# A joined state-space convolution and multi-query attention kernel: the start reordered, two rounds of scores over three key blocks put ahead of two projection steps, allowance 1.80

## The chip, the cores and the metric

The kernel runs on one core of a Trainium2 chip. The time is device microseconds for one execution of the whole program, and the figure that counts is the median of several runs of the same program. Lower is better.

## The reference

Two independent results are computed and put side by side. The first (A) is a long convolution: a kernel K of 2048 taps is generated for each of 576 channels from complex exponentials over 128 states, the input u is convolved with it, and a skip term is added. The second (B) is attention with 32 query heads of width 18 and one shared key and value head, over 2048 positions.

```python
P = jnp.exp(logdA[:, :, None] * l[None, None, :])
K = jnp.einsum("dn,dnl,dn->dl", Cc, P, dB).real
...
y = irfft2(rfft2(pad(u)) * rfft2(pad(K)))[..., :L] + u * Dskip
...
q = (x @ wq).reshape(B, S, 32, 18)
k = x @ wk
v = x @ wv
scores = einsum("bhqd,bkd->bhqk", q, k) * 18 ** -0.5
o = einsum("bhqk,bkd->bhqd", softmax(scores), v)
b = o.reshape(B, S, 576) @ wo
return concatenate([a, b], axis=-1)
```

## The kernel before

Attention is the spine. The 2048 queries are cut into four chunks of 512, the heads into 16 pairs, the keys into 16 blocks of 128. One element of the list `pairs` is (chunk c, group g, key block kb, member j): head pair 2g+j against key block kb. For each element TensorE (PE) makes a tile of scores (`scores`, line 516: two matmuls, one per head, 128 keys by 512 queries), and ScalarE (ACT) turns it into exponentials P (`exponentials`, lines 525 and 527). For each two elements (one step, both members of a key block) PE multiplies P with the values (`product`, line 817: four matmuls into `ops`). There are 1024 elements and 512 steps. Scores go out in rounds of NS = 3 elements, because three PSUM tiles hold them; ten P tiles (NP) lie between exponentials and products. Line 525 is the first group of chunk 0, which uses a bias.

Queries and keys are made as fp16 high and low parts with 55 rows for a pair member (18 high, 18 high, 18 low and one row for a bound). The queries of a pair stand in `aug`, the keys in `kaug`, 512 columns for each chunk of positions. `place` writes six small DMAs of 18 rows to fill one chunk of `kaug`.

The convolution is a second list of work (class Conv) whose VectorE (DVE) and PE instructions are put between those of attention. DVE makes tables of powers, PE generates K from them (`kg`), both u and K go through a transform on PE (`hu`, `hk`, `lu`, `lk`), DVE multiplies, PE transforms back (`iy`), and SP stores the result `outa`. There are twelve chunks of channels; chunk k+1's first half (`front`) runs beside chunk k's second half (`back`).

The order of PE, ACT and DVE is the order in which the program emits instructions (`manual_schedule`); the tile framework orders the other engines' queues, GpSimd's (POOL) among them. The emission follows a planner in `main`: a Clock keeps a rough account of each engine's time, and after each round `fill` places other work on PE: query projections, output projections and convolution. How far the convolution may run is an allowance: with `work` as the DVE time that the planner has booked for it, `lag = step * RATE - work`; below -20 nothing more is emitted, and a positive lag lets DVE be booked up to 1 us further ahead. `lags` puts the convolution ahead of the query projections while `work < step * PACE`.

The start is in `setup` (lines 234 to 344). It loads the first chunk of x (`x0`, five pieces of 128 input channels), the other three chunks (`xr`, five pieces), the query weights `wq[0]`, the key and value weights `wkv` and tables. Then:

- "first": the queries of heads 0 to 6 and the keys of chunk 0, five accumulation steps over k.
- ACT makes `h1` (high part), DVE `l1` (low part). `place(0)` and twelve DMAs from line 322 fill `kaug` chunk 0 and `aug[0]`, `aug[1]`.
- `rest(k)`, k = 0 to 4: the keys of chunks 1 to 3 and the last queries into "second", the values into "vps". Between the first of them the bias is made (`small`).
- Three matmuls over zeros (`spare`, from `wo`).
- DVE makes `h2` and `l2` from "second", and `place(1)` fills `kaug` chunk 1, on SP and POOL; then the values are copied (`vt`).

In `main`, after the first round of scores (r = 0), `settle` transposes the values into `v_sb`, places `kaug` chunks 2 and 3 on SP, loads `wq[2]` to `wq[4]` and starts the convolution's larger loads. After the third round (r = 6) `bounds` makes the limits `kmx` of the key blocks, which the later queries wait for.

Of the kernel before, what the change touches and what calls it, by code (L numbers as in the profile page):

```python
# [17 lines left out]
P = 128  # L18
# [3 lines left out]
DH = 18  # L22
SCALE = DH ** -0.5
NCH = 4
CT = 512
# [17 lines left out]
NS = 3  # L43
NP = 10


RATE = 1.84
PACE = 1.79
# [147 lines left out]
class Attention:  # L196
# [36 lines left out]
    def setup(self, tp, conv):  # L233
# [29 lines left out]
        nc.scalar.dma_start(self.wq[0], a["wq"][0])  # L263
        nc.sync.dma_start(wkv, a["wkv"])
        for k in range(5):
            n = DT[k][1]
            nc.sync.dma_start(x0[:n, k, :], a["xT"][0, :n, k, :])
        nc.scalar.dma_start(self.sel, a["sel"][:, 0:45])
        nc.scalar.dma_start(spread[:, 0:140], a["sel"][:, 45:185])
        for k in range(5):  # L270
# [5 lines left out]
        self.load_wq(1)  # L276
# [11 lines left out]
        p1, small, spare = p1[:, 0, :], small[:, 0, :], small[:, 1, 0:256]  # L288
        V.memset(self.wo[:, 0, 0:384], 0.0)
# [26 lines left out]
        self.place(0, h1, l1, 96, (nc.sync, nc.sync))  # L316
        for pr in range(2):
            for row, src in ((0, h1), (18, h1), (36, l1)):
                for j in range(2):
                    h, b = 2 * pr + j, 64 * j + row  # L320
                    q = nc.sync if pr and row == 36 else nc.gpsimd
                    q.dma_start(self.aug[pr][b:b + 18, :], src[h * DH:h * DH + DH, :])
# [18 lines left out]
        V.tensor_copy(vt, pv)  # L341
        V.tensor_reduce(self.km[:, 4:5], p2, axis=AX.X, op=ALU.max, apply_absolute_value=True)
        V.tensor_scalar(self.km[:, 4:5], self.km[:, 4:5], QS, None, op0=ALU.mult)
        self.vt = vt
# [412 lines left out]
    def main(self, conv, flag):  # L757
# [9 lines left out]
        pairs = [(c, g, kb, j) for c in range(NCH) for g in range(8) for kb in range(16) for j in range(2)]  # L767
        state = dict(credit=0.0, filled=0.0)
# [41 lines left out]
        def product(n):  # L810
            nonlocal o_ps
            c, g, kb, _ = pairs[2 * n]
# [3 lines left out]
            for j in range(4):  # L816
                nc.tensor.matmul(o_ps[32 * j:32 * j + 32, :], self.v[:, kb, :], pts[2 * n + j // 2][:, j % 2, :],  # L817
                                 start=(kb == 0), stop=(kb == 15), tile_position=(0, 32 * j))
            K.pe(0.88, done[2 * n + 1] + 0.1, self.o_free if kb == 0 else 0.0)
# [749 lines left out]
```

## Time and profile before

| what | value |
|---|---|
| median of 3 runs | 1157.36 us (1155.91 to 1157.46) |
| the profiled execution | 1158.43 us |
| its span, first to last instruction | 1156.7 us |
| PE busy | 1083.0 us (94%) |
| ACT busy | 998.6 us (86%) |
| DVE busy | 995.8 us (86%) |
| POOL busy | 141.5 us (12%) |
| mean granted TensorE clock | 0.993 |

The span is one execution; the 1.7 us between it and the time of that execution lie outside the first and last instruction. PE time is counted by matmul records. An fp32 matmul makes two records, an fp16 one makes one. Four matmuls of 32 output columns that stand side by side in the array are four instructions and run together, so that their records overlap.

### The profile page before, as it was taken

The numbers are of one execution on the slowest core, as the hardware profiler recorded it, in microseconds if no ns is written. First come the engines' busy times: TensorE is split into PE (matmuls) and PEld (weight loads), VectorE is DVE, ScalarE is ACT, GpSimd is POOL, SyncE is SP. The second block draws the span as 40 slices with busy tenths as digits, with TensorE's granted clock in tenths as the row PEclk, the third lists the DMA queues.
The fourth block names the chain that finished last, engine by engine and source line by source line (L and its number), as shares of the span: only waits on it lengthen the run. The fifth ranks groups of instructions, "written<-read, shape, count | busy, mean of one in ns | idle before, by whom it ended". The sixth has DMA issues, their size and how long they took to land.

```text
span 1156.7 us, 33067 instructions
## 1 busy us (share of the span) xinstructions
PE 1083.0 (94%) x13886; PEld 393.1 (34%) x13886; DVE 995.8 (86%) x1739; ACT 998.6 (86%) x1052; POOL 141.5 (12%) x257
## 2 busy tenths in 40 slices
PE   6999899999999999899999999989999999999997
PEld 1333333324334333323333333334323333323323
DVE  3788996998998998898899798997898899799683
ACT  3889998888888998998898989887999989899992
POOL 5321322022022000001022000001050000000000
PEclk9999999999999999999999999999999999999999
DMA  7412331114123102112222302102122200311101
GB/s 226 140 46 73 125 119 50 52 42 143 36 74 101 40 28 93 58 40 87 82 85 77 104 21 74 48 29 91 46 84 77 87 30 29 105 48 47 58 29 58
DMA packets 58751, 83.37 MB, mean 72 GB/s; under 512 B 14467, under 2 KB 34679, under 8 KB 58085
## 3 DMA queue, kind: packets, MB, share of 16 engines
q1 hardware_dynamic: 47173, 73.39, 19.2%
q0 software_dynamic: 10848, 7.37, 2.5%
q8 instruction: 111, 1.82, 0.6%
q10 hardware_dynamic: 576, 0.43, 0.2%
q14 instruction: 43, 0.35, 0.1%
HBM read 46.59 MB, written 33.85 MB: 70 GB/s over the span
## 4 chain that ended last, share of the span: by engine, by line
PE 59%; DVE 21%; ACT 12%; issue 6%; DMA 1%; POOL 1%; ACTq 0%; DVEq 0%; POOLq 0%
PE ops L817 24%; PE s L516 15%; ACT P L527 11%; PE op L193 5%; PE q L408 4%; DVE tab L119 4%; PE iy L193 3%; DVE ks L119 3%; PE kg L1253 3%; DVE acc L119 2%; DVE t L119 2%; PE hu L193 1%; PE hk L193 1%; DVE fr L119 1%; PE fin L193 1%
## 5 line engine op out<-in xcount | busy, mean ns | idle before, releaser
L527 ACT ACTIVATE P<-s 128x1024 f32<-128x1024 f32 x992 | 934.6, 1033 | 113.8 <-PE s L516 111.5
L817 PE MATMUL ops<-P,v_sb 128*32 128x512 f32 x4096 | 510.4, 599 | 8.1 <-DVE o L123 7.8
L516 PE MATMUL s<-aug,kaug 55*128 55x512 f16 x2048 | 308.2, 381 | 37.3 <-ACT P L527 33.4
L516 PEld LDWEIGHTS <-kaug 55*128 55x128 f16 x2048 | 91.0, 94 | 372.3 <-issue 326.7
L817 PEld LDWEIGHTS ops<-P,v_sb 128*32 128x32 f32 x4096 | 117.0, 110 | 164.8 <-issue 128.3
L458 POOL DMA_DIRECT2D qd<-qh x116 | 65.6, 572 | 309.6 <-DVE qh L127 307.0
L408 PE MATMUL q<-x,wq_sb 128*32 128x256 f32 x1360 | 83.7, 382 | 0.1
L193 PE MATMUL op<-wo_sb,oT 126*32 126x288 f32 (+1 forms) x1080 | 78.5, 416 | 2.6 <-DVE ob L123 1.4
L119 DVE TENSOR_TENSOR tab<-tab,tt 128x576 f32<-128x576 f32 (+1 forms) x72 | 59.1, 821 | 1.4
L119 DVE TENSOR_TENSOR tab<-tab 128x576 f32<-128x576 f32 (+1 forms) x72 | 58.8, 817 | 0.0
L119 DVE TENSOR_TENSOR tab<-fr,dif 128x576 f32<-128x576 f32 (+1 forms) x72 | 58.8, 817 | 0.0
L119 DVE TENSOR_TENSOR tt<-fr,sum 128x576 f32<-128x576 f32 (+1 forms) x72 | 58.8, 817 | 0.0
L119 DVE TENSOR_TENSOR tab<-sum,fr 128x576 f32<-128x576 f32 (+1 forms) x72 | 58.8, 817 | 0.0
L123 DVE COPY ksb<-kg 128x192 f32<-128x192 f32 x48 | 17.5, 364 | 46.9 <-PE kg L1253 46.6
L408 PEld LDWEIGHTS q<-x,wq_sb 128*32 128x32 f32 x1360 | 39.4, 109 | 38.5 <-issue 13.9
L119 DVE TENSOR_TENSOR acc<-acc,pt 128x1728 f32<-128x1728 f32 (+2 forms) x36 | 48.7, 1352 | 0.1
L119 DVE TENSOR_TENSOR pt<-us,ks 128x1728 f32<-128x1728 f32 (+2 forms) x36 | 48.4, 1351 | 0.1
L1162 POOL MEMSET fr<- 128x192 f32 x24 | 11.9, 580 | 294.0 <-DVE tt L119 192.2
L193 PEld LDWEIGHTS op<-wo_sb,oT 126*32 126x32 f32 (+1 forms) x1080 | 30.6, 110 | 44.2 <-issue 18.3
L525 ACT ACTIVATE P<-s,bias 128x1024 f32<-128x1024 f32 x32 | 32.8, 1123 | 12.9 <-PE s L516 12.7
L1253 PEld LDWEIGHTS kg<-tab 128*32 128x32 f32 x2304 | 35.7, 110 | 22.7 <-DVE ksb L123 7.6
L1253 PE MATMUL kg<-tab 128*32 128x64 f32 x2304 | 41.8, 220 | 1.2 <-DVE tab L119 0.8
(160 smaller groups left out, 1022.4 us busy)
## 6 DMA issues: line engine op xcount, KB each, us to landing
od<-o SPq DMA_DIRECT2D x31, 256.0 KB
aug<-qd SPq DMA_DIRECT2D x124, 55.0 KB
u<-u SPq DMA_DIRECT2D x12, 384.0 KB
kd<-ksb SPq DMA_DIRECT2D x12, 384.0 KB
kt<-kd SPq DMA_DIRECT2D x48, 96.0 KB
outa<-u SPq DMA_DIRECT2D x12, 384.0 KB
pw<-pw SPq DMA_DIRECT2D x8, 528.0 KB
oT<-od SPq DMA_DIRECT2D x16, 252.0 KB
```

Source lines behind the costliest of these rows:

```text
L119: return self.v.tensor_tensor(out, *a, **k)
L123: return self.v.tensor_copy(out, *a, **k)
L193: nc.tensor.matmul(ps[j:e], w[:, j:e], x, start=start, stop=stop, tile_position=(0, j))
L408: nc.tensor.matmul(ps[o, 256 * f:256 * f + 256], w[:, k, i], xt[:, k, x], start=(k == 0), stop=(k == 4), tile_position=(0, 32 * j))
L458: q.dma_start(qd[h:h + n, row + d:row + d + nd, cs], src[i1:i1 + n * nd, :cs.stop - cs.start])
L516: nc.tensor.matmul(ps[:, j, :], self.kaug[r, kb * P:(kb + 1) * P], t[r, :], start=True, stop=True)
L525: nc.scalar.activation(pt, ps, AF.Exp, bias=self.bias, scale=SCALE / QQ)
L527: nc.scalar.activation(pt, ps, AF.Exp, scale=SCALE / QQ)
L817: nc.tensor.matmul(o_ps[32 * j:32 * j + 32, :], self.v[:, kb, :], pts[2 * n + j // 2][:, j % 2, :], start=(kb == 0), stop=(kb == 15), tile ...
L1162: nc.gpsimd.memset(t[:, :, 0:NF:8], one)
L1253: nc.tensor.matmul(ps[32 * g:32 * g + 32, d, :], t[:, :32], t[:, 32:], start=(j == 0), stop=(j == 1), tile_position=(0, 32 * g))
```

## The change

The changed program does the following.

- Loads: `wq[0]` goes first on ACT's queue, the first piece of `x0` first on SP's, then `wkv`, then the other pieces of `x0` in two DMAs with all 128 rows (the padding rows come from the host's array, and the memset of them goes). The convolution's first parameters follow on ACT's queue and on POOL's, `sel` and `spread` on POOL's.
- `xr` pieces 0 to 2 are loaded as before, pieces 3 and 4 and `wq[1]` only after the DMAs that place `h1` and `l1`; a memset of one element on DVE ahead of each makes it wait there.
- Four matmuls over zeros (`WARM`) stand at the start, the three `spare` ones go. The memsets of `ring` move from POOL to DVE.
- The low part's two DMAs into `kaug` chunk 0 go to ACT's queue; all twelve `aug` DMAs go to POOL's.
- `rest(3)` moves behind the first round of scores, `rest(4)` and the making and placing of `h2`, `l2`, `vt` (`keys_rest`) behind the second. `settle` comes after the third round, `bounds` after the fifth.
- The first six elements of `pairs` are reordered: key blocks 0, 1, 2 of pair 0, then of pair 1. `place`, `member` and `exp` keep the products in step with it.
- Three more parts of the convolution's first chunk are emitted in `setup` (`conv.begin(3)`).
- POOL's order, too, is that of the program.
- RATE 1.84 becomes 1.80, PACE 1.79 becomes 1.75.

```diff
-RATE = 1.84
-PACE = 1.79
+WARM = 4
+RATE = 1.80
+PACE = 1.75
...
-        nc.gpsimd.memset(x0[64:, 4, :], 0.0)
+        V.memset(self.wo[:, 0, 0:384], 0.0)
         nc.gpsimd.memset(xr[64:, 4], 0.0)
-        for j in range(2):
-            nc.gpsimd.memset(self.ring[j], 0.0)
+        nc.scalar.dma_start(self.wq[0], a["wq"][0])
+        nc.sync.dma_start(x0[:, 0, :], a["xT"][0, :, 0, :])
+        nc.sync.dma_start(wkv, a["wkv"])
+        nc.sync.dma_start(x0[:, 1:3, :], a["xT"][0, :, 1:3, :])
+        nc.sync.dma_start(x0[:, 3:5, :], a["xT"][0, :, 3:5, :])
         conv.early()
...
+        for k in range(3):
+            load_rest(k)
...
+        warm = self.bank(256, "warm")
+        for _ in range(WARM):
+            matmul4(nc, warm, self.wo[:, 0, 0:P], self.wo[:, 0, P:P + 256])
+        for j in range(2):
+            V.memset(self.ring[j], 0.0)
...
-        self.place(0, h1, l1, 96, (nc.sync, nc.sync))
+        for row, src in ((0, h1), (36, h1), (18, l1)):
+            for j in range(2):
+                b = 64 * j + row
+                (nc.scalar if row == 18 else nc.sync).dma_start(self.kaug[b:b + 18, 0:CT], src[96:96 + 18, :])
...
+        for k in range(3, 5):
+            V.memset(xr[0:1, k, :, 0:1], 0.0)
+            load_rest(k)
+        V.memset(self.wq[1][0:1, 0, 0:1], 0.0)
+        self.load_wq(1)
...
-        for k in range(2, 5):
-            rest(k)
-        for _ in range(3):
-            matmul4(nc, spare, self.wo[:, 0, 0:P], self.wo[:, 0, P:P + 256])
+        rest(2)
+        conv.begin(3)
+        self.rest_of, self.p2_p3, self.vt = rest, (p2, pv), vt
+
+    def keys_rest(self):
...
+        pairs[0:6] = pairs[0:6:2] + pairs[1:6:2]
...
             if r == 0:
+                self.rest_of(3)
+                K.t += 1.9
+                continue
+            if r == NS:
+                self.rest_of(4)
+                self.keys_rest()
+                K.t += 1.9
+                continue
+            if r == 2 * NS:
                 self.settle(conv)
-            if r == 2 * NS:
+            if r == 4 * NS:
                 self.bounds()
...
-        with tc.manual_schedule(engines={mybir.EngineType.PE, mybir.EngineType.Activation, mybir.EngineType.DVE}):
+        with tc.manual_schedule(engines={mybir.EngineType.PE, mybir.EngineType.Activation, mybir.EngineType.DVE, mybir.EngineType.Pool}):
```

More of the change, by code (lines that the diff above doesn't have):

```diff
@@ L287, in setup @@
         p1, small = (self.ps_s.tile([P, 2, CT], F32, tag="s", name=n) for n in ("first", "small"))
[L288 to L289 removed]
+        p1, small, spare = p1[:, 0, :], small[:, 0, :], None
         p2 = self.bank(CT, "second")
@@ L320, in setup @@
                     h, b = 2 * pr + j, 64 * j + row
-                    q = nc.sync if pr and row == 36 else nc.gpsimd
-                    q.dma_start(self.aug[pr][b:b + 18, :], src[h * DH:h * DH + DH, :])
+                    nc.gpsimd.dma_start(self.aug[pr][b:b + 18, :], src[h * DH:h * DH + DH, :])
+        for k in range(3, 5):
[3 more added lines that the diff above has]
+        self.load_wq(1)
         V.tensor_scalar(self.km[:, 0:1], ab[:, 0:1], spread[:, 139:140], None, op0=ALU.mult)
@@ L767, in main @@
         pairs = [(c, g, kb, j) for c in range(NCH) for g in range(8) for kb in range(16) for j in range(2)]
+        pairs[0:6] = pairs[0:6:2] + pairs[1:6:2]
+        place = {x: i for i, x in enumerate(pairs)}
+        member = lambda i: 16 * (8 * pairs[i][0] + pairs[i][1]) + pairs[i][2]
+        exp = lambda n, j: place[n // 128, n // 16 % 8, n % 16, j]
         state = dict(credit=0.0, filled=0.0)
@@ L840, in main @@
             for i in new:
-                while (i - NP) // 2 >= behind:
+                while i >= NP and member(i - NP) >= behind:
                     product(behind)
@@ L845, in main @@
                 c, g, kb, j = pairs[i]
-                pts[i] = self.exponentials(i, c, 2 * g + j, kb, *ss[i], read.get((i - NP) // 2, 0.0))
+                pts[i] = self.exponentials(i, c, 2 * g + j, kb, *ss[i], read.get(member(i - NP), 0.0) if i >= NP else 0.0)
                 done[i] = K.a
@@ L1115, in powers @@
         if g == 0:
-            for k in (1, 2):
-                self.load(k)
             yield "v", K.v + 0.3, False
@@ L1185, in factors @@
         w = self.coefficients(k)
-        if k > 0:
-            self.load(k + 2)
+        for j in (k + 2,) if k else (1, 2):
+            self.load(j)
         if k + 1 == BURSTS[g][1]:
```

37 lines of the change are left out of this document (19 added, 18 removed).

## The prediction

> **What bounds the kernel now.** I read the page first, then a table of windows, then the timeline and the chain of waits of the start.
>
> ```profile
> span 1156.7 us, 33067 instructions
> ...
> PE 1083.0 (94%) x13886; PEld 393.1 (34%) x13886; DVE 995.8 (86%) x1739; ACT 998.6 (86%) x1052; POOL 141.5 (12%) x257
> ```
>
> ```profile
> 0.00:14.00 14.00, 6.03 (x44) 1.39 (x48) 3.42 (x9) 3.91 (x5) 4.72 (x11) 1.00 0.80 253
> 14.00:26.30 12.30, 10.81 (x114) 3.42 (x106) 4.86 (x13) 2.69 (x4) 8.27 (x17) 1.00 0.77 232
> 26.30:36.00 9.70, 7.56 (x54) 3.01 (x50) 5.51 (x27) 9.16 (x9) 7.55 (x14) 0.91 0.28 76
> 46.00:60.00 14.00, 13.90 (x172) 4.80 (x168) 11.86 (x20) 12.12 (x13) 5.59 (x10) 1.00 0.35 105
> ...
> 200.00:400.00 200.00, 189.27 (x2530) 70.28 (x2524) 184.23 (x344) 176.01 (x188) 32.82 (x60) 1.00 0.23 71
> ```
>
> The columns are the window, its length, busy time of PE, weight loads, DVE, ACT and POOL, the granted clock, the DMA share and GB/s. Later PE is full: 13.90 of 14 us, then 95% of 200. In the first 36 us it idles 8.0, 1.5 and 2.1 us, and an idle microsecond there is one at the end, as the work left is the same. So I follow the start to a landmark, the end of the fourth round of scores, where two products are done and PE is full:
>
> ```profile
> 36.55 1.37 PE L516 MATMUL s<-aug,kaug 55*128 55x512 f16 x6
> ```
>
> It began at 36.55 and ended at 37.92. Before it:
>
> ```profile
> 0.75 4.01 DMA pos_sb<-pos
> ...
> 4.78 2.79 DMA x<-xT
> ...
> 7.62 1.07 PE first L294 x3
> ...
> 9.55 0.85 PE first L294 x3
> ...
> 11.32 0.43 PE first L294 x3
> ...
> 13.55 0.61 ACT keys L311
> ```
>
> ```profile
> 14.74 4.02 POOL L322 DMA_DIRECT2D aug<-keys  x8 [9.41 <-ACT keys L311]
> ...
> 23.18 0.63 PE L298 MATMUL second<-xr,wkv_sb 128*32 128x512 f32 x3 [0.25 <-DMA xr<-xT]
> ...
> 24.30 0.69 DVE L127 TENSOR_SCALAR keys<-second 128x512 f16<-128x512 f32 x1 [5.75 <-PE second L294]
> ...
> 24.89 1.50 PE L193 MATMUL small<-wo_sb 128*32 128x256 f32 x24
> ...
> 26.33 1.04 PE L516 MATMUL s<-aug,kaug 55*128 55x512 f16 x6
> ...
> 26.78 9.16 ACT L525 ACTIVATE P<-s,bias 128x1024 f32<-128x1024 f32 x9 [9.72 <-PE s L516]
> ```
>
> The first x piece is issued at 4.78, held by the landing of another load, and lands at 7.57. "First" then runs to 13.5, its rows 0.85 apart until 10.4 and 0.43 apart later (two rows to a k). The last pieces of the other chunks arrive at 23.18, the zeros take 1.50, and the first scores go at 26.33. From there ACT sets the pace: nine exponentials in 9.16, and PE waits for its PSUM tiles.
>
> **The change part by part.** *x first.* In the first 40 us the loads are limited by what the DMA engines move (GB/s for each microsecond, so KB):
>
> ```profile
> GB/s 0 4 41 128 334 297 296 293 330 356 317 360 391 391 385 383 383 391 281 203 258 220 156 23 43 72 94 56 67 40 31 63 34 302 84 18 52 20 169 293
> ```
>
> Before, 1007 KB are issued up to the first x piece (24+48+96 parameters, 11 pos, 160 wkv, 320 wq, 92 tables, 256 x). The row adds up to that at 6.7, and the piece lands at 7.57, 0.9 later. Now 736 KB (x, wq, wkv) suffice: 5.8 + 0.9 = 6.7. All of x with those small loads is 2031 KB: 9.9 + 0.9 = 10.8, and the two steps of k that arrive last take 2 x 0.86, so "first" ends at 12.5 instead of 13.5. Bounds: 11.0 (6.7 and ten rows of 0.43), 13.5 (nothing gained). I take 1.0 sooner, by the bytes. The WARM matmuls lie in the 7.6 us that PE idles at the start; they bring the 0.43 pace from the first step, which the bytes then hide.
>
> *h1 and aug.* h1 is then done at 13.1 and l1 1.3 later. POOL issues at 0.5 each (4.02 for eight), four high rows from 13.7, then two low: the sixth, the last that pair 0 needs, at 16.2. Time to landing:
>
> ```profile
> DMA to landing us min/median/max: 4.2/6.4/7.0
> ```
>
> ```profile
> DMA to landing us min/median/max: 1.7/1.9/3.4
> ```
>
> The first row is POOL's aug under the load of xr, the second its kaug later, when the engines move little. xr pieces 0 to 2 are now 2031 + 2304 KB, which the GB/s row reaches at 16.1; so the sixth flies as the load ends. Between 1.7 and 7.0 I take 3.0: it lands at 19.2. rest(2) needs xr 2 at 17.0 (16.1 + 0.9) and is done at 18.8, within that. First scores at 19.2 rather than 26.33.
>
> The Trainium skill (page "DMA: Bandwidth & Descriptors", section "Anatomy of one DMA — SWDGE (gpsimd) path") puts a DMA of POOL at about 2.0 us and its bytes over 436 GB/s, so 2.0 for 18 KB; the trace agrees for kaug (1.9) and not for aug (6.4). By that rule the scores would start 1.0 us sooner.
>
> *From there on.* Three scores take 1.0, a rest 1.8 (twice the matmuls of a k of "first", so four rows of 0.43). Scores to 20.2; rest(3) to 22.0 (its xr lands near 19 if the rate holds, SP issues it after four kaug at 0.7 from 13.1); scores of member 1 to 23.0; rest(4) to 24.8. Then h2 and l2 as before, 24.8 to 26.2, and `kaug` chunk 1:
>
> ```profile
> L350 SPq DMA_DIRECT2D kaug<-keys x21: 697/707/926, 14.2 to 36.3; - x21
> ```
>
> Three issues of 0.7 on SP after h2, the last no sooner than l2: 26.9; with 1.9 to land, 28.8. The ninth score (key block 4) needs it. What stands behind it on PE is the transposing of the values (`settle` now comes after it), so every product waits for it, and ACT, with eight exponentials done by about 27.6, runs dry. Transposing to v_sb:
>
> ```profile
> 27.30 0.66 PE L359 MATMUL vp<-ident,keys 128*128 128x128 f32 x4
> ...
> 27.99 0.46 DVE L123 COPY v_sb<-vp 128x288 f32<-128x288 f32 x1
> ...
> 34.68 1.94 PE L817 MATMUL ops<-P,v_sb 128*32 128x512 f32 x8
> ```
>
> 1.15 us: 28.8 + 0.4 + 1.15 = 30.35. Two products at 0.86 to 1.9 each (the second is the row at 34.68) and three scores at 0.8 to 1.37 follow: 32.9 to 35.5, I take 34.2 against 37.92, so 3.7 gained.
>
> *bounds.* The kmx matmuls (12, 1.30 us in the chain's row below) leave the stretch before the landmark and come after it, at the warm pace about half: 0.7 to pay later. The chain behind them (up, sh, the fetch of the next queries) is 3 us later; sh was issued at 43.0 for a pair due at the 33rd element, which ACT cannot reach before 28.8 + 24 x 1.02 = 53, so some 7 us of cover stay.
>
> ```profile
> 33.45 1.30 PE kmx L382 x12
> ...
> 43.79 2.30 PE q L408 x40
> ```
>
> ```profile
> 29.08 0.70 DVE L119 TENSOR_TENSOR pw<-pw,m 128x528 f32<-128x528 f32 x1
> 29.81 1.15 DVE L123 COPY fr<-pw 128x192 f32<-128x192 f32 x6
> ...
> 43.02 0.59 POOL L496 DMA_DIRECT2D qd<-sh  x1 [9.17 <-DVE sh L127]
> ```
>
> *At nothing:* the ring memsets (DVE is busy 3.42 of the first 14 us), conv.begin(3) (the 1.4 and 1.15 us of DVE below, in the 5.75 that it waited before h2), the two DMA issues on ACT (idle 9.72 before the exponentials), raw and tables on POOL's queue (POOL waited 9.41 for h1), wq[1] some 6 us later (needed at 43.79), `kaug` chunks 2 and 3 placed three rounds later: chunk 2 is six SP issues of 0.7 from 30.4, there at 36.5, and due at the 17th element, no sooner than eight exponentials of 1.02 after the ninth, 37.4; that cover is thin, and a late one would stall PE by the difference. POOL in program order puts place(1) ahead of the qd stores, which is better for it. Each of these costs its own duration on the path if its cover is gone.
>
> Sum: 3.7 - 0.7 = 3.0 us less. In the profiled execution that is 1158.43 - 3.0 = 1155.4; the median of the runs stands 1.07 below that execution, so **1154.4**. Bounds of the start, kmx counted: POOL's landings at 1.7 and warm products give 5.6 gained; at 7.0 and cold products 2.3 lost.
>
> The Trainium skill (page "TensorE: Matmul & The Clock Gate", section "Part 1: The HAM clock gate (the "warmup" mystery)") states that an idle window of about 3.4 us returns PE to half speed. The windows show 0.91 after the sparse stretch, and the product at 34.68 takes 1.94. PE's new wait for kaug chunk 1 (24.8 to 28.8, with two scores in it) is of that length, so by that rule the products are cold, the landmark is at 35.5, and 1.3 us of the lead go.
>
> **The rivals.** *A, a larger lead:* POOL's landings come at kaug's 1.9 and the products are warm: about 5.5 gained, 1151.9. For it: less is in flight. Against: xr still loads until 16.
>
> *B, the lead is given back* at the keys of chunk 1: aug lands at 6.4 as before and the products are cold. The scores start at 22.6, the ninth at 32.2, the landmark lies at 38.9, 1 us late, and with kmx 1159.1; with one of the two, about 1156. For it: 6.4 is the median of that very DMA. Against: the engines' load is moved to later.
>
> *C, slower: the convolution is late at the end.* By the planner's own costs (0.075 + 0.11 if it reads the last output + elements by rate) the twelve chunks are booked at about 930 us. At the last step, 511, the old allowance is 1.84 x 511 = 940, the new one 920. If the convolution follows it, its last part is 20 / 1.84 = 11 steps late. What remains is emitted after the loop, ahead of the last output projection.
>
> ```profile
> 1072.53 0.34 SPq L536 DMA_DIRECT2D od<-o  x1
> ...
> 1106.59 0.35 SPq L536 DMA_DIRECT2D od<-o  x1
> ...
> 1129.92 0.37 SPq L1410 DMA_DIRECT2D outa<-u  x1
> ```
>
> ```profile
> 1124.79 1.44 PE iy L193 x32
> ...
> 1127.84 1.44 PE iy L193 x32
> ...
> 1136.26 2.91 PE fin L193 x48
> ```
>
> 16 steps take 34.1 us, so 11 are 23; the last store is at 1129.9 and `fin` starts at 1136.3, 6.3 us of slack. 17 us remain; without rounds between, the chain runs at half its length (the iy are 3.05 apart and 1.44 long), 8.5 us: 1154.4 + 8.5 = 1162.9. It decides from three steps of lateness (6.3 / 2.13). Against it: 2.5 us of it are now done in `setup`, and the allowance only slows the booking, it doesn't stop it above -20.
>
> **How the numbers follow.** Forecast 0.42, A 0.14, B 0.16, C 0.28. 0.2% is 2.3 us, about what this kernel's measurement can tell from none: faster is below 1155.0, slower above 1159.7. A changed order also moves PE's other idle time (10.7 us of the 200 shown, some 54 in the body); I allow 4 us either way, so the forecast's own range is 1150 to 1158, and of its 0.42 I give 0.29 to faster, 0.11 to same, 0.02 to slower. A is all faster; B 0.02, 0.09, 0.05; C 0.02 same, 0.26 slower. Sum: faster 0.45, same 0.22, slower 0.33. The range runs from 1148 (the 5.6 of the best start with the 4 of the body) to 1163 (C).
>
> **What would show it.** The first scores near 19 (before 26.33), the ninth near 29, the landmark near 34; DMA times of aug near 3. A clock below 0.8 in the windows about 30 is the cold stretch. C shows as an `outa` store after the last `ops`, with PE idle ahead of `fin`. I am wrong if the landmark is not sooner, or if it is and the end doesn't follow it, which would mean that PE alone isn't the bound.

## The result, and the profile after

The changed kernel takes 1160.35 us (median of 12 runs, 1159.40 to 1162.32) against 1157.09 for the kernel before in the same session: a ratio of 1.0032, 95% interval 1.0023 to 1.0041. It is 0.3% slower, where the forecast was 3 us faster. The profiled execution took 1160.5 us.

The first two lines of its page:

```profile
span 1158.6 us, 33102 instructions
...
PE 1083.3 (93%) x13894; PEld 394.0 (34%) x13894; DVE 998.9 (86%) x1751; ACT 999.1 (86%) x1052; POOL 142.6 (12%) x259
```

PE's busy time is the same within 0.3 us, so most of the 1.9 us of span is idle time of PE (73.7 before, 75.3 after). A table of windows cut at two landmarks shows where. The landmarks are SP's issues that fetch a finished group of outputs (`od<-o`), the first and the last of 31. The columns are those of the windows above. The kernel before:

```profile
0.00:68.59 68.59, 56.66 (x604) 19.16 (x608) 42.72 (x103) 44.04 (x45) 28.57 (x56) 0.98 0.53 163
68.59:1106.59 1038.00, 984.22 (x12800) 357.85 (x12792) 925.22 (x1593) 927.90 (x979) 112.94 (x202) 1.00 0.21 67
1106.59:1156.70 50.11, 42.12 (x503) 16.07 (x502) 27.89 (x44) 26.64 (x30) 0.00 (x0) 0.97 0.14 50
```

The changed kernel:

```profile
0.00:77.08 77.08, 60.91 (x622) 20.61 (x626) 44.11 (x113) 43.76 (x45) 31.40 (x60) 0.93 0.49 148
77.08:1106.29 1029.21, 979.14 (x12772) 357.08 (x12774) 916.89 (x1580) 928.18 (x978) 111.18 (x200) 1.00 0.21 68
1106.29:1158.60 52.31, 43.27 (x508) 16.28 (x504) 37.92 (x59) 27.19 (x31) 0.00 (x0) 0.97 0.14 48
```

The start, up to the first gather, is 8.5 us longer. The body makes 8.8 of it up, and the tail is 2.2 longer. PE's idle time (the window less PE's busy time) goes from 11.9 to 16.2 in the start, from 53.8 to 50.1 in the body and from 8.0 to 9.0 in the tail: 4.2 more, 3.7 less, 1.1 more. The lengths themselves say less, since the changed kernel does more work ahead of its first gather (622 matmul records against 604). So two things of opposite sign lie behind a small result, and the experiments have to part them.

The start, first. In the timeline of the kernel before, ACT's row ahead of h1:

```profile
8.85 0.64 ACT L1108 ACTIVATE pw<-pw 128x528 f32<-128x528 f32 x1 [2.71 <-DVE pw L127]
```

The timeline of the changed kernel from there on (start, length, engine, line; in brackets the idle time of the engine before the row, and what ended it):

```profile
10.92 0.63 PE L299 MATMUL first<-x,wq_sb 128*32 128x512 f32 x3 [0.39 <-DMA x<-xT]
...
11.80 0.26 DVE L120 TENSOR_TENSOR ab<-ab,dt 128x96 f32<-128x96 f32 x1 [9.70 <-DMA ab<-pa]
...
12.23 0.61 PE L299 MATMUL first<-x,wq_sb 128*32 128x512 f32 x3
...
14.88 0.64 ACT L1141 ACTIVATE pw<-pw 128x528 f32<-128x528 f32 x1 [6.15 <-DVE pw L128]
15.43 0.58 ACT L316 ACTIVATE keys<-first 128x512 f16<-128x512 f32 x1
...
16.30 6.01 POOL L329 DMA_DIRECT2D aug<-keys  x12 [10.87 <-ACT keys L316]
...
17.70 0.38 PE L338 MATMUL small<-km,spread_sb 128*128 128x1 f32 x2 [2.51 <-DVE km L128]
...
19.22 1.06 PE L303 MATMUL vps<-x,wkv_sb 128*32 128x512 f32 x1
...
20.07 1.06 PE L303 MATMUL vps<-x,wkv_sb 128*32 128x512 f32 x1
...
23.34 0.82 PE L531 MATMUL s<-aug,kaug 55*128 55x512 f16 x6
...
28.20 0.98 PE L531 MATMUL s<-aug,kaug 55*128 55x512 f16 x6 [1.30 <-DMA aug<-keys]
...
30.25 0.69 DVE L128 TENSOR_SCALAR keys<-second 128x512 f16<-128x512 f32 x1 [5.50 <-PE second L299]
...
34.70 0.50 PE L531 MATMUL s<-aug,kaug 55*128 55x512 f16 x2 [3.12 <-DMA kaug<-keys]
...
35.84 0.46 DVE L124 COPY v_sb<-vp 128x288 f32<-128x288 f32 x1 [2.00 <-PE vp L374]
...
36.36 3.23 PE L836 MATMUL ops<-P,v_sb 128*32 128x512 f32 x16 [0.55 <-DVE u L1070]
39.52 0.82 PE L531 MATMUL s<-aug,kaug 55*128 55x512 f16 x6
```

"First" ends at 12.84 instead of 13.47, 0.6 us sooner where 1.0 was wanted. But ACT has a Sin of the convolution's tables ahead of h1 in its order. Before, that Sin ran at 8.85, long before "first" was done. Now it runs at 14.88, because its inputs are loaded behind `wq[0]` and, with x, arrive at 11.8 and 12.4. So h1 starts 1.9 us later than before instead of sooner. PE then waits 2.51 us for DVE's work on the same input (the row at 17.70), and behind that wait the granted clock is 0.50 to 0.52 from 18.5 to 22.0: the rows at 19.22 and 20.07 are 0.85 apart, where a row takes 0.43 at a granted clock of 1.00. And the second round of scores does not follow rest(3): it waits for `aug` of the other pair. The chain of waits has both (start, length, what):

```profile
2.41 9.96 DMA pos_sb<-pos
...
14.88 0.64 ACT pw L1141
15.53 0.49 ACT keys L316
...
17.84 3.47 POOL aug L329 x7
21.31 6.84 DMA aug<-keys
28.16 0.05 issue
28.20 0.98 PE s L531 x6
```

The fourth round of scores ends at 40.34, 2.4 us later than before. From there to the first gather another 6.1 us are lost, and the timeline shows how:

```profile
43.45 1.27 PE L397 MATMUL kmx<-km,spread_sb 128*128 128x4 f32 x12
...
52.65 2.37 PE L423 MATMUL q<-x,wq_sb 128*32 128x256 f32 x40
...
62.33 0.31 PE L194 MATMUL up<-sel_sb,aw 128*32 128x8 f32 x16 [2.54 <-DVE aw L128]
...
63.06 3.13 ACT L540 ACTIVATE P<-s,bias 128x1024 f32<-128x1024 f32 x3 [4.49 <-PE s L531]
```

The limits `kmx` come two rounds later by the code and 10 us later in time (33.45 before), the next query projection starts at 52.65 instead of 43.8, and its limits (`up`) stand in PE's order ahead of the next scores. PE waits 2.5 us for them, and ACT 4.5 us for scores.

### The profile page after: what moved, and what is told of

The parts are those of the page before. It is cut to its first block, busy times and chain, and to the rows that moved or that the text cites. A ratio compares the mean times of both kernels' runs of the same rounds, so it can differ in the third digit from the quotient of the medians.

```text
span 1158.6 us, 33102 instructions
## 1 busy us (share of the span) xinstructions
PE 1083.3 (93%) x13894; PEld 394.0 (34%) x13894; DVE 998.9 (86%) x1751; ACT 999.1 (86%) x1052; POOL 142.6 (12%) x259
## 4 chain that ended last, share of the span: by engine, by line
PE 66%; DVE 14%; ACT 12%; issue 5%; DMA 2%; POOL 0%; ACTq 0%; DVEq 0%
PE ops L836 27%; PE s L531 17%; ACT P L542 12%; PE q L423 5%; PE op L194 5%; PE kg L1284 3%; PE iy L194 3%; DVE tab L120 2%; DVE ks L120 2%; PE hu L194 1%; PE hk L194 1%; DVE stage L120 1%; DVE acc L120 1%; PE fin L194 1%; PE lk L194 1%
## 5 line engine op out<-in xcount | busy, mean ns | idle before, releaser
L423 PEld LDWEIGHTS q<-x,wq_sb 128*32 128x32 f32 x1360 | 40.8, 110 | 43.1 <-issue 18.5
```

What stands on the lines that cost most here:

```text
L423: nc.tensor.matmul(ps[o, 256 * f:256 * f + 256], w[:, k, i], xt[:, k, x], start=(k == 0), stop=(k == 4), tile_position=(0, 32 * j))
```

## The experiments

"Ratio" is to the kernel before in the same session, with its 95% interval. The last four columns come from each kernel's own trace: the start of the first scores, the first gather, the time from the first to the 31st gather, and from there to the end of the span.

| kernel | median us | ratio | first scores | first gather | body | tail |
|---|---|---|---|---|---|---|
| before | 1157.09 | 1 | 26.33 | 68.59 | 1038.00 | 50.11 |
| after | 1160.35 | 1.0032 [1.0023, 1.0041] | 23.34 | 77.08 | 1029.21 | 52.31 |
| after_again | 1161.60 | 1.0034 [1.0021, 1.0048] | 23.24 | 76.72 | 1030.47 | 52.11 |
| a_old_allowance | 1182.27 | 1.0226 [1.0211, 1.0241] | 22.70 | 76.59 | 1047.09 | 58.22 |
| b_new_allowance | 1191.72 | 1.0312 [1.0296, 1.0327] | 25.77 | 67.06 | 1030.16 | 90.78 |
| b_delay | 1162.05 | 1.0056 [1.0042, 1.0069] | 30.86 | 73.21 | 1036.54 | 49.95 |
| a_h1_first | 1160.16 | 1.0039 [1.0024, 1.0054] | 20.94 | 75.28 | 1029.24 | 52.88 |
| a_bounds2 | 1158.01 | 1.0016 [1.0007, 1.0024] | 23.13 | 73.65 | 1029.23 | 53.22 |
| a_fix | 1156.12 | 1.0002 [0.9993, 1.0011] | 20.94 | 72.14 | 1029.14 | 52.22 |
| a_xr_late | 1164.95 | 1.0071 [1.0055, 1.0086] | 22.98 | 79.39 | 1029.16 | 52.25 |
| a_no_rounds | 1159.41 | 1.0015 [1.0006, 1.0025] | 28.50 | 70.81 | 1036.10 | 49.89 |
| b_rounds | 1161.41 | 1.0035 [1.0021, 1.0048] | 24.92 | 75.68 | 1030.69 | 52.33 |
| a_18025 | 1160.80 | 1.0034 [1.0021, 1.0047] | 23.48 | 76.83 | 1029.50 | 51.87 |
| a_no_iy | 1158.09 | 1.0003 [0.9993, 1.0013] | 21.52 | 77.98 | 1030.44 | 48.88 |
| b_no_iy | 1156.30 | 0.9984 [0.9973, 0.9995] | 25.66 | 69.55 | 1036.59 | 49.46 |
| b_1825 | 1151.18 | 0.9959 [0.9943, 0.9974] | 24.63 | 65.83 | 1030.62 | 51.15 |
| n_best | 1152.86 | 0.9963 [0.9951, 0.9974] | 25.85 | 70.91 | 1031.25 | 51.24 |

The last four columns are one execution each, and kernels with the same start program show how far these differ: the first gather lies at 65.83 to 69.55 in four traces of the old start (before, `b_new_allowance`, `b_1825`, `b_no_iy`) and at 76.59 to 77.98 in five of the changed one (after, `after_again`, `a_old_allowance`, `a_18025`, `a_no_iy`). A difference of 1 us between two such rows means little; the 8.5 us above is far beyond it.

### The allowance and the start exchanged

`a_old_allowance` is the changed kernel with the old allowance, `b_new_allowance` the kernel before with the new one.

```diff
-RATE = 1.80
-PACE = 1.75
+RATE = 1.84
+PACE = 1.79
```

> The changed kernel with RATE 1.84 and PACE 1.79 as before; the start stays as changed. Theory C (the lower allowance makes the convolution late, and its last iy behind the loop cost the 3.3 us): the last outa store comes before the last products again and the time goes back to about 1157. Theory S (the start loses, its 8.5 us at the first gather come back at the end): no change, 1160, within 1. Theory O (the allowance steers an order whose end is hard to foresee): counting what the program emits, 7.0 us of booked DVE work stand behind the loop here against 1.1 with 1.80, so the last outa store is later than 1140.3 and the time is 1163 or more.

> The kernel before with RATE 1.80 and PACE 1.75, nothing else. Theory C: the convolution is late here too. The program emits 32 us of booked DVE work behind the loop (0 before), so the time is 15 to 30 us more, 1172 to 1187. Theory S: the allowance has no part, 1157 within 1.

Measured: 26 us and 35 us slower than the kernel before. The three windows of `b_new_allowance` end with this one:

```profile
1097.22:1188.00 90.78, 55.57 (x848) 24.85 (x847) 64.70 (x103) 27.68 (x31) 0.00 (x0) 0.81 0.12 41
```

PE is busy for 55.57 of 90.78 us there, DVE for 64.70: a part of the convolution's last chunk is left behind the loop, where nothing runs beside it. The timeline has PE's longest wait of that stretch:

```profile
1163.63 2.78 PE L193 MATMUL iy<-w,dft_sb 128*32 128x192 f32 x32 [21.76 <-DVE w L119]
```

This is rival C's picture, with the lower allowance on the old start. `a_old_allowance`, the higher one on the new start, loses in another place: its body is 17.9 us longer than the changed kernel's and its tail 5.9. So the allowance is no dial with a direction. A small step of it gives another order of all the work, and 1.80 is one that suits the new start. It is worth 22 us against 1.84 there.

### Does a later start come out at the end?

`b_delay` is the kernel before with 15 matmuls over zeros in place of the three ahead of h2.

```diff
-        for _ in range(3):
+        for _ in range(15):
             matmul4(nc, spare, self.wo[:, 0, 0:P], self.wo[:, 0, P:P + 256])
```

> The kernel before with 15 matmuls over zeros instead of 3 ahead of the first scores: 12 more at 0.43 to 0.50, 5.2 to 6 us of PE in the start, the order of everything else the same. If an idle or lost microsecond of the start comes back one for one, the time is 5 to 6 us more, 1162.5 to 1163. If the body takes it up in its own idle time (53 us of PE between 80 and 1100), it is 0 to 3 more.

Measured: the first scores are 4.5 us later, the first gather 4.6 later, the time 5.9 us longer by medians (4.9 to 8.0 by the interval). By the medians, a loss at the start is not made up by the body if the order of the body stays. The single traces are looser: `fin`, the last projections, starts only 3.2 us later than in the kernel before's trace, whose body of 1038.00 is the longest of its order (`b_delay`, `a_no_rounds` and `b_no_iy` have 1036.1 to 1036.6; PE's idle time in it is 53.7 to 53.9 in all four). The table says the same of all kernels that have the changed kernel's order: their bodies take 1029.1 to 1030.7 us, whatever the start.

### h1 ahead of the Sin

`a_h1_first` puts five of the six early steps of the convolution behind h1 and l1, the Sin among them.

```diff
-        conv.begin(6)
+        conv.begin(1)
...
-        conv.begin(4)
+        conv.begin(9)
         rest(0)
```

> The changed kernel with five of the convolution's first six parts emitted behind h1 and l1 instead of ahead, so that h1 on ACT does not stand behind the first Sin, which waits for late parameters. h1 starts at 12.7 instead of 15.43. Theory S: first scores about 2 us sooner, first gather and the end 2 to 2.7 us sooner, 1158. Theory C: the end stays, 1160 within 1, as the loop's last step and the two iy behind it set it.

Measured: h1 starts at 12.92 instead of 15.43, the first scores are 2.4 us sooner, the fourth round 1.8, the first gather 1.8 (1.3 below the least of the five traces above), and `fin` 1.8. PE's granted clock is 1.00 from 18 to 22 here. The second round still waits for aug, 1.76 us, until 25.73. In the medians the 1.8 us are not resolved by this run alone (1.0039 with an interval of 0.3% against 1.0032).

### The bounds back to the second round

`a_bounds2` undoes one line.

```diff
-            if r == 4 * NS:
+            if r == 2 * NS:
                 self.bounds()
```

> The changed kernel, with the bounds put back to where the kernel before has them (behind the second round of scores, not the fourth); nothing else is changed. Theory 1 (the late bounds, not the landmark, set the first half of what is lost up to the first gather: the fourth round was 2.4 us late, the first gather 8.5): kmx and the projection of the next queries come some 6 us sooner, PE's wait near 60 us goes, and the first gather is at 72 to 74 us instead of 77; the body then has less to make up, and the time falls by up to 4 us, to 1157 to 1159, if the order of the rest stays. Theory 2 (PE is what counts and the order of the body makes up whatever the start lost): the first gather is sooner, and the end stays at 1160 to 1161, with fin at 1139 to 1141. Theory 3 (the bounds are where they are because they stand in the way of the scores): the fourth round of scores is 1.2 us later and the first gather no sooner than 77.

Measured: the first gather at 73.65, 3.4 us sooner, and the last projections (`fin`) start at 1136.10 instead of 1139.50, also 3.4 sooner. The time falls to 1158.01, ratio 1.0016. Theory 1 is right in place and size. The fourth round of scores itself comes 2.4 us later (41.88 against 39.52), as the third theory had it (with half the size), but that delay is not what the end hangs on.

### Both mends together

`a_fix` has both edits.

> The changed kernel with both mends together: the Sin of the convolution's tables behind h1 and l1 on ACT's order, and the bounds back to behind the second round of scores. Theory 1 (each passes one for one to the end as long as the order of the body stays): first scores at 21, first gather at 71.9 (77.1 less 1.8 less 3.4), last outa store near 1135, 1156 to 1158 and a ratio of 0.999 to 1.001. Theory 2 (what counts is the allowance's order, the start hardly): 1158 to 1160, like either mend alone.

Measured: first scores 20.94, first gather 72.14, `fin` at 1134.49: 4.9 us sooner at the gather and 5.0 at the end, the sum of the two within 0.3. By medians 1156.12, ratio 1.0002, where the changed kernel has 1.0032 and 1.0034. So these two causes hold the whole loss against the kernel before. They don't hold the gain that was forecast: the second round still waits 1.65 us for aug, until 25.54, and no run has h1, the bounds and aug all in time. The windows of `a_fix`:

```profile
0.00:72.14 72.14, 61.12 (x622) 21.02 (x626) 43.91 (x113) 43.73 (x45) 32.15 (x62) 0.93 0.52 159
72.14:1101.28 1029.14, 979.13 (x12772) 357.07 (x12774) 916.48 (x1580) 928.16 (x978) 110.62 (x198) 1.00 0.22 68
1101.28:1153.50 52.22, 43.26 (x508) 16.27 (x504) 37.92 (x59) 27.20 (x31) 0.00 (x0) 1.00 0.14 48
```

The body and the tail have the same counts of instructions as the changed kernel's, and the same times to 0.1 us. PE's idle time in the start is 11.0 instead of 16.2 (11.9 in the kernel before).

### Why aug's rows land late

`a_xr_late` is the changed kernel with the loads of the last two pieces of the other chunks' x, and of `wq[1]`, held until POOL has issued its last aug row.

```diff
-            V.memset(xr[0:1, k, :, 0:1], 0.0)
+            nc.gpsimd.memset(xr[0:1, k, :, 0:1], 0.0)
             load_rest(k)
-        V.memset(self.wq[1][0:1, 0, 0:1], 0.0)
+        nc.gpsimd.memset(self.wq[1][0:1, 0, 0:1], 0.0)
```

> The changed kernel with the loads of the last two pieces of the other chunks' x, and of the next query weights, held until POOL has issued the last aug row (they waited for first's reader before). Theory 1 (aug's rows land after 6.8 us because these loads fill the engines): every aug row lands within 2 to 3 us of its issue; the second round of scores no longer waits for aug, but rest(3) now waits for x, so that the start as a whole is later, and the time 1161 to 1164. Theory 2 (a row issued by POOL behind many others lands late whatever else is loaded): the last rows of aug still take 5 to 7 us, and the second round goes at 28 or later because of them.

Measured, for the tile `aug`, in the changed kernel:

```profile
L329 POOL DMA_DIRECT2D aug<-keys x12: 505/505/536, 16.3 to 21.8; - x12
...
DMA to landing us min/median/max: 1.7/1.9/7.1
```

and in `a_xr_late`:

```profile
L329 POOL DMA_DIRECT2D aug<-keys x12: 507/507/562, 16.0 to 21.6; - x12
...
DMA to landing us min/median/max: 1.6/1.8/2.6
```

The issues are the same; only the loads beside them differ, and the longest landing falls from 7.1 to 2.6. Theory 1 holds: the rows are late because of what SP issued from 19.34 on, the two pieces of x and then `wq[1]`. The run holds all three back and does not say which of them counts most. The second round now waits for x instead, its chain has

```profile
22.26 4.76 DMA xr<-xT
```

and it starts at 30.28, not at 28.20; the time is 4.6 us longer than the changed kernel's by medians of different sessions (a ratio of 1.0071 against 1.0032). Either aug waits for x or x for aug: the second round needs both.

### One part alone

`a_no_rounds` keeps the new loads, queues and warm-up and has the old order of scores, bounds, keys and allowance.

```diff
-        rest(2)
-        conv.begin(3)
...
+        for k in range(2, 5):
+            rest(k)
...
-        pairs[0:6] = pairs[0:6:2] + pairs[1:6:2]
...
-            if r == 0:
-                self.rest_of(3)
...
-            if r == NS:
-                self.rest_of(4)
-                self.keys_rest()
```

> The changed kernel's loads, queues, warm matmuls and POOL order with the main part of before: rest(3), rest(4) and keys_rest ahead of the first scores, pairs, settle, bounds and the allowance as before, no conv.begin(3). So the order behind the first scores is that of before, and any change is the start's. Theory S: h1 at 15.4 instead of 13.55 and late pieces of xr put the first scores at 28 to 31 instead of 26.33, and the end is later by the same, 1159 to 1161. If the loads alone are a gain (as the prediction had it), the first scores are sooner than 26.3 and the time is below 1157.

Measured: 1159.41, ratio 1.0015. The loads alone lose: rest(3) waits 2.71 us for x in the trace, since its pieces 3 and 4 are held until h1, and h1 starts at 15.54 here too. First scores 28.50, 2.2 us later than before.

`b_rounds` is the other half: the old loads, the two rounds ahead of rest(3) and rest(4), the bounds in their old place, and the allowance of 1.80, so that the body has the changed order.

```diff
-        for k in range(2, 5):
-            rest(k)
+        rest(2)
+        conv.begin(3)
...
+        pairs[0:6] = pairs[0:6:2] + pairs[1:6:2]
...
+            if r == 0:
+                self.rest_of(3)
+            if r == NS:
+                self.rest_of(4)
+                self.keys_rest()
```

> The kernel before with its own loads, but with the two rounds of scores ahead of the last two steps of k, the bounds in their old place, and the change's allowance of 1.80 (1.75), which gives it the same order of work in the body as the changed kernel with its bounds put back. Theory 1 (the rounds ahead win little, since the second round waits for the other pair's aug rows, which POOL issues last and which land late; the loads lose about 1.7 us): first scores at 22 to 25, second round 3 us or more behind them, fourth round at 37 to 39, 1155 to 1157.5, below the 1158.0 of the changed kernel with its bounds put back. Theory 2 (the two parts need each other: with the old loads the third step of x's other chunks comes at 23 anyway): first scores at 25 or later, and no sooner at the fourth round than the changed kernel; 1158 to 1161.

Measured: 1161.41, near Theory 2 by the numbers, but not for its reason: the first scores at 24.92 wait 4.70 us for aug and not for x. The median landing of aug is 6.3 under the old loads. The same order of work with the new loads, queues and warm-up is `a_bounds2`, which has its first gather 2.0 us sooner (73.65 against 75.68) and a ratio of 1.0016 against 1.0035. So the new loads help the rounds ahead and hurt without them, and neither half gains alone.

### What is left behind the loop

In the changed kernel two `iy` blocks of the last chunk stand behind the last product, ahead of `fin`:

```profile
1136.02 1.48 PE L194 MATMUL iy<-w,dft_sb 128*32 128x192 f32 x32
1138.18 1.51 PE L194 MATMUL iy<-w,dft_sb 128*32 128x192 f32 x32 [0.68 <-DVE u L120]
1139.50 3.10 PE L194 MATMUL fin<-wo_sb,oT 126*32 126x288 f32 x48
```

`after_again` repeats the changed kernel beside the kernels of this group. `a_no_iy` and `b_no_iy` are the two kernels without the last chunk's `iy` blocks and the sums behind them.

```diff
-                    matmul4(nc, ps[:, r % 2, :], self.dft[:, q * P:(q + 1) * P], w[:, 4 * j + r, :], start=(j == 0), stop=(j == 1))
+                    if k < NCK - 1:
+                        matmul4(nc, ps[:, r % 2, :], self.dft[:, q * P:(q + 1) * P], w[:, 4 * j + r, :], start=(j == 0), stop=(j == 1))
```

> The changed kernel as it is, beside the others of this call on the same chip: every theory expects 1.003 of the kernel before, about 1160.

> The changed kernel without the last chunk's transform back (its two iy blocks on PE, 3.0 us, and the two adds behind them are left out, so the last 48 channels of the convolution are wrong; everything else is in the same order). Theory C: both blocks stand behind the loop and ahead of fin, so fin starts at 1136.0 instead of 1139.5 and the time is 3.3 to 3.5 us less than the changed kernel's, 1157. If fin waits for something else as well, less.

> The kernel before with the same part left out. There both blocks stand between the last rounds of scores. Theory C says that they cost little there, since ACT sets the pace of the last 30 us (a round of three exponentials takes 3.03 us and three of them 2.85 to 3.1): 0 to 1 us less, 1156. If PE sets the pace there, 3 us less, and then C is no cost of the place: both kernels pay the blocks in full.

Measured: the repeat agrees with the first result. Without the blocks the changed kernel is 3.5 us faster, the kernel before 1.4. The difference of 2.1 looks like the price of having them behind the loop. The next run speaks against that.

`a_18025` is the changed kernel with an allowance of 1.8025.

```diff
-RATE = 1.80
-PACE = 1.75
+RATE = 1.8025
+PACE = 1.7525
```

> The changed kernel with an allowance of 1.8025 (and pace 1.7525) instead of 1.80 (1.75); the start's program is the same. Theory 1 (what is left over behind the loop costs 3.5 us here, since the two last iy blocks stand between the last store and fin): by the code's own booking nothing is left over, the iy blocks stand ahead of the last store, and fin starts at once behind it; 1157 to 1159, some 2 us less. Theory 2 (the order that comes out is a matter of luck in the body): the leftover is gone and yet the time is anywhere from 1155 to 1175, as the body's own pace changes with each step of the allowance; the 31st gather then is more than 3 us off 1106.5.

Measured: the blocks are inside the loop again, the last convolution store and `fin` come sooner, and the time does not move: 1160.80, ratio 1.0034. Theory 1 misses. The time lies in the wide range of Theory 2, but its sign doesn't come: the 31st gather is at 1106.33, as in the changed kernel, and only the order of the tail changes:

```profile
1133.68 0.86 PE L194 MATMUL iy<-w,dft_sb 128*32 128x192 f32 x16
...
1135.19 0.37 SPq L1441 DMA_DIRECT2D outa<-u  x1
1136.93 3.10 PE L194 MATMUL fin<-wo_sb,oT 126*32 126x288 f32 x48
```

The two blocks are 3 us of PE's work wherever they stand: PE idles 9.0 us in the tail of the changed kernel and 9.2 in this one, so their place behind the loop costs it nothing that can be seen. Why leaving them out gains more in the changed kernel than in the kernel before stays open, as does where the tail's remaining 1 to 2 us against the kernel before come from.

### Better than both

`b_1825` is the kernel before with an allowance of 1.825 (pace 1.775). `n_best` has in addition the new loads with h1 ahead of the Sin and all five pieces of x loaded at the start.

```diff
-RATE = 1.84
-PACE = 1.79
+RATE = 1.825
+PACE = 1.775
```

> The kernel before with an allowance of 1.825 (pace 1.775) instead of 1.84 (1.79), nothing else. By the code's own booking nothing is left over and the end comes 2.5 us sooner. Theory 1 (the booking foretells the order's worth where nothing is left over): 1154 to 1156, a ratio of 0.997 to 0.999. Theory 2 (the allowance must match the start, and 1.84 is already at its best for the old start): 1157 to 1162 or worse. The first gather stays at 68 to 70 in both, since the allowance hardly acts in the first 60 us.

> The changed kernel's loads without its two rounds ahead: before's order of scores, the bounds and the key blocks in their old places; x first, wkv and wq as in the change; but the Sin of the convolution behind h1 and l1 on ACT's order, all five pieces of the other chunks' x loaded at the start (none held back until h1), and an allowance of 1.825. Theory 1 (what the new start lost is h1 behind the Sin, and the late pieces 3 and 4 of x, 1.8 us in all): h1 near 13, first scores at 24.5 to 26, ahead of before's 26.3, and 1153 to 1156. Theory 2 (the loads' order itself loses, since every byte is needed by the first scores anyway): first scores at 26.3 or later and 1157 to 1160.

Measured: `b_1825` takes 1151.18, ratio 0.9959 (0.9943 to 0.9974), the fastest of all here, without any change to the start. Its windows:

```profile
0.00:65.83 65.83, 55.06 (x604) 19.31 (x608) 42.73 (x103) 44.06 (x45) 28.60 (x56) 1.00 0.56 170
65.83:1096.45 1030.62, 980.04 (x12794) 357.97 (x12783) 919.45 (x1588) 927.72 (x979) 113.36 (x202) 1.00 0.22 68
1096.45:1147.60 51.15, 42.78 (x506) 16.08 (x503) 33.72 (x50) 27.05 (x31) 0.00 (x0) 1.00 0.14 49
```

PE's idle time in the body is 50.6 instead of 53.8, a gain like the one that the changed kernel has in its body (50.1), to be had with the allowance alone. The start's program is the same as before, so the earlier first gather (65.83 against 68.59) is one execution's. `n_best` has the same ratio within its interval, its first scores are at 25.85 as Theory 1 had it, though h1 starts at 14.39 and not near 13, and its first gather (70.91) is later than that of `b_1825`: the new loads, mended, gain nothing over the old ones.

## Why the prediction was wrong

The sum of 3.0 us had three kinds of terms: a landmark 3.7 sooner, 0.7 for kmx, and nothing for the rest. Step by step, in us:

| step | forecast | measured | off by |
|---|---|---|---|
| "first" ends | 12.5 | 12.8 | 0.3 |
| h1 done | 13.1 | 16.0 | 2.9 |
| first scores | 19.2 | 23.3 | 4.1 |
| second round | 22.0 | 28.2 | 6.2 |
| h2 | 24.8 | 30.25 | 5.4 |
| ninth score | 28.8 | 34.7 | 5.9 |
| v_sb made | 30.35 | 36.3 | 6.0 |
| fourth round ends | 34.2 | 40.3 | 6.1 |

**x first: right.** The sum of bytes over the row of GB/s put the last pieces of x at 10.8, and PE's row that waits for them starts at 10.92. The end of "first" came out to 0.3 us.

**"h1 is then done at 13.1": the first wrong step.** It took "first" for h1's only condition. ACT runs in program order, and `conv.begin(6)` had put a Sin ahead of h1. In the kernel before that was free, since the parameters came first. The change's other half moved just those parameters behind `wq[0]`, and the prediction has no term for that: among the things at nothing it names `raw` and the tables on POOL's queue, and not the parameters on ACT's. `a_h1_first` shows it: with the Sin behind, h1 starts at 12.92, 0.4 after the 12.5 of the forecast.

**First scores at 19.2: 1.2 more were lost behind h1.** The prediction timed rest(2) by x alone. The two small matmuls of the bias stand between the rests in PE's order and wait for DVE's work on h1's input, 2.51 us in the row at 17.70. The slow clock behind that wait added to it, some 0.4 us for each of four rows. It does not follow every time: in `a_no_iy`, whose start is the same, PE waits 2.43 us, the granted clock stays at 1.00, and the first scores are at 21.52. The second round goes at 27.93 there all the same, since aug sets it. With h1 in time the first scores are at 20.94, 1.7 later than forecast. There PE waits 1.58 us for DVE, which now has the convolution's steps ahead of `aw_first`:

```profile
19.02 0.24 PE L194 MATMUL small<-sel_sb,aw_first 128*32 128x4 f32 x8 [1.58 <-DVE aw_first L128]
```

**"Scores of member 1 to 23.0": a wait that was left out.** The aug rows of pair 0 were followed one by one; those of pair 1 have no term in the sum at all. They are six issues of 0.5 further down the same queue, and the last were issued just when x pieces 3 and 4 loaded. They landed after up to 7.1 us, and the second round stood 6.2 us late. `a_xr_late` shows the cause. The 3.0 taken for a landing was too long for pair 0, whose rows went late enough to have little beside them (the median is 1.9), and far too short for pair 1. With h1 in time it is too short in general: in `a_h1_first` the landings take 2.8 to 6.3 us, 4.5 in the median.

**From h2 to the landmark: right.** From the second round on, every step lies 5.4 to 6.2 us behind its forecast, so the distances held: kaug took 1.89 to land in the chain, with 1.9 forecast. The two products were slow: they took 3.23, at a granted clock of 0.50 from 36.3 to 38.0, behind PE's wait of 3.12 for kaug. Two later ones took 1.92:

```profile
46.46 1.92 PE L836 MATMUL ops<-P,v_sb 128*32 128x512 f32 x16
```

The sum had 2.76 for the two, the middle of its bounds. The scores behind them ran at 0.82, near the lower bound, so that only 0.2 of the 1.3 us that the prediction's cold case adds was lost. The rule of the Trainium skill that the prediction drew on (page "TensorE: Matmul & The Clock Gate", section "Part 1: The HAM clock gate (the "warmup" mystery)") puts PE at half speed after an idle window of about 3.4 us. The trace agrees on the half speed, but here it came behind waits of 2.13 (`a_old_allowance`), 2.51 and 3.12 us and not behind the 2.43 of `a_no_iy`, so the length of the wait alone does not tell.

**"Some 7 us of cover" behind the bounds: wrong.** The estimate compared the fetch of the next queries with the element that needs them. The step that binds is another: the next query projection on PE cannot start before the limits, and `up` of that projection then stands in PE's order ahead of scores. It came 9 us later, PE waited for it, and 3.4 us of start were lost. `a_bounds2` gives them back, to the end. The 0.7 for the kmx matmuls was too small as well: they take 1.27 in the row at 43.45, with the granted clock at 1.00, so the 1.30 of the kernel before was no slow pace to be halved.

**"The end follows the landmark": right, for one order of the body.** `b_delay`, `a_h1_first`, `a_bounds2`, `a_fix` and `a_xr_late` show it in both directions, `b_delay` by its median and the last four to 0.2 us from the first gather to `fin`. It does not hold across the allowance.

**The allowance at nothing, with 4 us either way, or rival C with 8.5 lost: the first mis-sized, the second wrong.** It won. The body has 3.7 us less idle time of PE, which lies just within the 4 us, and with the new start the old allowance costs 22 us more. `b_1825` shows that a like gain can be had with the old start. C's reasoning (so many steps late, so long a chain behind the loop) foresaw the place, two `iy` blocks behind the last product, but not the amount: 3 us of matmuls, and `a_18025` got no time back by moving them into the loop.

**The rivals.** B was the nearest: aug at 6.4, products cold, landmark at 38.9 and 1159.1, against a landing of 6.84, cold products, 40.3 and 1160.35. Its lateness at the keys was right. It had one pair's rows late rather than the other's, and lacked h1 and the bounds; the gain in the body hid most of those. That its time came within 1.3 us is luck: too little loss in the start and no gain in the body. A, and the 1.0 us for quicker landings, counted too much by the prediction's own working, which has rest(2) done at 18.8: a quicker landing could bring the first scores forward by 0.4 and no more.

## What to carry to other kernels

When a load is moved back, look up every reader of it, and then what stands behind that reader on its engine: here a Sin of another part of the program, moved by nobody, held h1. When a round needs several small transfers, give each its own term, its place in the queue and what else loads at that time; the last one issued decides. Where the order of the work comes out of a planner, change the allowance alone on the old kernel before crediting the change with what a new allowance brings. And before a difference of 1 or 2 us between two traces is explained, see how far traces of the same program lie apart.

## What the runs showed of the hardware

- An 18 KB row issued by POOL landed in 1.6 to 2.6 us with the large loads held back (`a_xr_late`) and in up to 7.1 us while two pieces of x (768 and 384 KB) and the next query weights loaded (`after`). The Trainium skill's figure (page "DMA: Bandwidth & Descriptors", section "Anatomy of one DMA — SWDGE (gpsimd) path"), 2.0 us, fits the former alone.
- With the same program order, the body repeated from run to run to 0.1 us in five traces (`after`, `a_h1_first`, `a_bounds2`, `a_fix`, `a_xr_late`: 1029.14 to 1029.24) and was 1.2 to 1.3 us longer in two others, the repeat of the first (1030.47) and `a_no_iy` (1030.44).
- With the same start program and nearly the same wait of PE (2.51 and 2.43 us), the granted clock from 18.5 to 22.0 was 0.51 in `after` and 1.00 in `a_no_iy`, and the first scores went at 23.34 and 21.52.
- PE's busy time differs for the same number of matmul records (13886): 1083.0 us in the trace of the kernel before at a mean granted clock of 0.993, 1077.9 in that of `b_1825` at 0.998. So 5 of the 9.1 us between these two spans are busy time and go with the granted clock, and the 4.7 us of the ratio are nearer to the difference in idle time (73.7 against 69.7).
